# Reordering the start and the background work of a fused Fourier-mixing and MLP kernel

## The chip, the cores and the metric

The kernel runs on one core of a Trainium2 chip. The metric is device time in microseconds (us), of which less is better. Before the change it took 1956.89 us, the median of three runs (1955.35 to 1957.33). Every run of this case was in the fast state, so none had to be put aside. Profiled spans are about 1.8 us shorter than the times of the same executions (1954.8 against 1956.62 before, 1950.6 against 1952.35 after). I compare times with times and spans with spans.

Engine names in the profile: PE is TensorE, PEld is TensorE's weight load (it overlaps PE: before, they were busy for 1719.2 and 1935.8 us of a span of 1954.8), DVE is VectorE, ACT is ScalarE, POOL is GpSimd, SP is SyncE, which issues most transfers (939 of the 944 in the trace of before). A q behind a name is that engine's sequencer.

## The reference

```python
def reference(x, w_in, w_out):        # x [8, 3008, 256], w_in [256, 2048], w_out [2048, 256]
    X = np.fft.fft(np.fft.fft(x, axis=1), axis=2).real   # mixing over sequence and features
    h = X.reshape(8 * 3008, 256) @ w_in
    return np.maximum(h, 0) ** 2 @ w_out                 # out [24064, 256]
```

## The kernel before

The kernel takes the eight sequences one after the other and calls each a block of work. For each it **folds** x on VectorE (sums and differences of mirrored rows and columns), so that the Fourier transform over the sequence becomes a few smaller products with cosine and sine tables; these give Pt, Qt and Et. P's folding uses sums (`f_s`), Q's uses differences (`f_d`). The transform over the features is multiplied into w_in beforehand (G1, G2, and a column gE). Then come 48 **steps** per sequence, 384 in all: each multiplies a slice of P and Q with G (`front`), squares the positive part (`combine`) and multiplies with w_out two steps later (`back`). A regular step has 11 products, each shown as two records of TensorE, and takes 4.67 us.

```python
def fold(b, t):                      # row tile t of sequence b; returns pieces (cost, function)
    def f_s(): ...                   # VectorE: fs = x[0::2] + x[1::2]
    def f_d(): ...                   # VectorE: fd = x[0::3] - x[1:3]; asks for a later x tile
    def f_sc(): ...                  # VectorE: half of fs     (P)
    def f_dc(): ...                  # VectorE: half of fd     (Q)
    def f_w(part): ...               # VectorE: sum and difference into w
    if b == 0:
        return [f_s, f_d, f_sc, f_dc, lambda: f_w(PART[0]), lambda: f_w(PART[1])]
    ops = [(0.9, f_s), (0.9, f_d), (0.7, f_sc), (0.6, f_dc), (1.1, f_w)]
    if not odd or t == ODD0:
        return ops
    ...
    def f_sine(): ...                # ScalarE: four scalings into f1, f2
    def f_odd():                     # VectorE: w = w * turn + f1 / f2, twice
        for nm, u in (("f1", "v"), ("f2", "w")):
            nc.vector.scalar_tensor_tensor(out=st[u][rows, 1], ..., in1=st[nm][rows], ...)
    return ops + [(0.8, f_turn), (1.3, f_even), (0.2, f_sine), (1.4, f_odd)]

def fold_columns():                  # only once, in the first sequence: the middle column of all others
    nc.scalar.mul(xe, xe, 2.0)
    ...                              # VectorE: es = xe + xe, we = es +- es

def front(b, k0, n, j, between):     # two halves h; each: two products, three evictions, then side work
    for h in range(2):
        nc.tensor.matmul(hP, G1[:, fs], pt[:, ks], ...)
        nc.tensor.matmul(hQ, G2[0:P - 1, fs], qt[:, ks], ...)
        nc.vector.scalar_tensor_tensor(out=t, in0=et[:, ks], scalar=gE[:, fc:fc + 1], in1=hP, ...)
        tt(out=g[:, h, 0], in0=t, in1=hQ, op=ALU.add)
        tt(out=g[:, h, 1][:, ::-1], in0=t, in1=hQ, op=ALU.subtract)
        between()

def between():                       # a gap: emit side work for the next sequence, by listed costs
    if i < 2 * NJ or i % NJ == LAG - 1:          # NJ = 8, LAG = 2
        return
    spent -= pace                                # pace = sum of the listed costs / number of gaps
    while side and spent <= 0:
        t, f = side.pop(0)
        f()
        spent += t

# the first phase, in the order in which it is emitted
awake(44)                            # unused products, meant to keep TensorE's clock up
for_p(0); for_q(0); for_p(1)         # for_p(t): f_s, f_sc, f_w ; for_q(t): f_d, f_dc, f_w
win = [load_win(0)]                  # w_in arrives in 64 bits; VectorE and ScalarE convert it (raw)
...                                  # loads of x tiles and tables
for_p(2); rounded(0); win[0][1](); awake(2); for_p(3); groups_at(0, 5)
awake(8); for_p(4); for_p(5); for_p(6)
groups_at(3, 8, 1, 2); for_q(4); ...             # groups_at: products of P, E, Q and their joins
groups_at(9, 13, 18, 11, 12, 16, 17); for_q(1); awake(8); groups_at(14, 23)
win.append(load_win(1)); groups_at(19, 28)
copy_e = win[0][2]()                 # small product pe on TensorE
for_q(2); for_q(3); groups_at(20, 25); awake(10)
copy_e()                             # VectorE: gE = pe * 0.5
...
```

The order of the Python calls is the order of the instructions on each engine: in `e8_pe_early` below, where VectorE's copy of pe is called ahead of a weight conversion, it runs at 37.11 us and the conversion at 37.80; in the kernel after it is called behind it and runs at 41.73, the conversion at 37.46. The listed costs only spread the side work over the gaps; they time nothing.

## Time and profile before

| stage of the span | us | what bounds it |
|---|---|---|
| first phase | 0 to 66 | x landing, then VectorE and TensorE (busy 23.70 and 23.76 us of the 25 from 25 to 50) |
| first steps, with w_in and w_out converted | 66 to 115 | TensorE full, VectorE close behind |
| steps with side work for the second sequence | 147 to 227 | TensorE, with losses |
| the other sequences | 252 to 1950 | TensorE full |

The prediction below shows the lines for most of this. Two views that it leaves out turned out to matter. The first is the page's list of the costliest groups (columns: line, engine, operation, output and inputs, count, then busy us and mean ns of one, then idle us just before them and what ended most of it):

```profile
L563 PE MATMUL ph<-Pt,G 128*128 128x251 f32 (+1 forms) x1536 | 453.2, 376 | 2.3 <-DVE g L569 1.6
...
L563 PEld LDWEIGHTS ph<-Pt,G 128*128 128x128 f32 x1536 | 287.4, 189 | 41.1 <-DVE g L569 5.4
```

The second is the view of waits between 147 and 232 us (total us, times, longest):

```profile
PEld ph L563 <- DVE g L569: 4.8, 8, 1.5
...
PE ph L563 <- DVE g L569: 1.6, 3, 1.1
...
DVE w L440 <- ACT f L426: 1.4, 1, 1.4
```

Both say that the weight load of a step's first product lost more to VectorE's eviction than the product itself: 5.4 against 1.6 us over the span, and eight waits against three in this stretch. Which row shows the loss more fully is the point on which the prediction's sum for this stretch went wrong.

### The profile page before, as it was taken

How to read it: one execution, taken by the hardware profiler on the slowest of the kernel's cores; microseconds unless marked ns; L12 is line 12 of the kernel's file. 1: busy time of each engine (PE TensorE's matmuls, PEld its weight loads, DVE VectorE, ACT ScalarE, POOL GpSimd, SP SyncE). 2: the span in 40 equal slices, each digit the busy share in tenths (PEclk: the TensorE clock that was granted, in tenths of full speed). 3: DMA queues.
4: the chain of work that ended last, by engine and by line, in shares of the span. 5: the costliest groups of instructions: out<-in, count | busy, mean ns of one | idle time of the engine just before them, and what ended most of it. 6: DMA issues, size and time to landing. Idle time of an engine off the chain costs nothing.

```text
span 1954.8 us, 27739 instructions
## 1 busy us (share of the span) xinstructions
PE 1935.8 (99%) x9272; PEld 1719.2 (88%) x9272; DVE 1405.2 (72%) x3442; ACT 925.3 (47%) x1068; POOL 1168.7 (60%) x1705
## 2 busy tenths in 40 slices
PE   8999999999999999999999999999999999999998
PEld 7888888888988899888988889888898888988887
DVE  8989967777677766777667776677767777655554
ACT  1754544455444444444444454444534454444443
POOL 0046645766567665666566665666756676566664
PEclk9999999999999999999999999999999999999999
DMA  7332102111111101111011100121001101100101
GB/s 198 108 37 57 35 11 54 33 27 28 23 37 41 37 13 27 41 39 29 11 35 38 44 19 11 40 49 27 20 16 51 33 12 22 27 11 12 22 11 22
DMA packets 145341, 68.90 MB, mean 35 GB/s; under 512 B 129003, under 2 KB 136110, under 8 KB 145197
## 3 DMA queue, kind: packets, MB, share of 16 engines
q1 hardware_dynamic: 144121, 66.60, 15.1%
q8 instruction: 73, 1.20, 0.3%
q10 hardware_dynamic: 1076, 0.52, 0.1%
q14 instruction: 71, 0.58, 0.1%
HBM read 42.39 MB, written 24.68 MB: 34 GB/s over the span
## 4 chain that ended last, share of the span: by engine, by line
PE 95%; DVE 3%; DMA 1%; ACT 1%; issue 0%; POOL 0%; SPq 0%; DVEq 0%; ACTq 0%
PE ph L563 16%; PE ph L564 16%; PE mC L616 16%; PE mA L616 16%; PE mB L616 16%; PE mD L616 8%; PE pd L465 3%; PE pd L512 2%; DMA xt<-in_x_dram 1%; PE mB L603 1%; PE mA L603 1%; PE pg L269 0%; DVE w L396 0%; DVE he L566 0%; DVE g L568 0%; DVE g L569 0%
## 5 line engine op out<-in xcount | busy, mean ns | idle before, releaser
L578 ACT ACTIVATE g<-g 128x1004 f32<-128x1004 f32 (+1 forms) x384 | 399.3, 1040 | 795.5 <-DVE g L569 393.8
L586 POOL TENSOR_TENSOR s<-g 128x251 f32<-128x251 f32 (+1 forms) x376 | 245.8, 654 | 711.3 <-ACT g L579 657.1
L566 DVE SCALAR_TENSOR_TENSOR he<-Et,gE,ph 128x251 f32<-128x251 f32 (+1 forms) x768 | 362.0, 471 | 415.3 <-PE ph L564 413.3
L563 PE MATMUL ph<-Pt,G 128*128 128x251 f32 (+1 forms) x1536 | 453.2, 376 | 2.3 <-DVE g L569 1.6
L564 PE MATMUL ph<-Qt,G 127*128 127x251 f32 (+1 forms) x1536 | 452.2, 375 | 0.9 <-DVE Qt L478 0.9
L579 ACT ACTIVATE g<-g 128x1004 f32<-128x1004 f32 (+1 forms) x384 | 399.3, 1040 | 12.1
L616 PE MATMUL mC<-s,wsum 128*128 128x251 f32 (+1 forms) x1504 | 381.4, 374 | 0.0
L616 PE MATMUL mA<-g,wout 128*128 128x251 f32 (+1 forms) x1504 | 379.9, 374 | 0.0
L568 DVE TENSOR_TENSOR g<-he,ph 128x251 f32<-128x251 f32 (+1 forms) x768 | 320.5, 417 | 55.1 <-POOL s L586 1.0
L564 PEld LDWEIGHTS ph<-Qt,G 127*128 127x128 f32 x1536 | 291.8, 190 | 37.2 <-DVE Qt L478 1.3
L563 PEld LDWEIGHTS ph<-Pt,G 128*128 128x128 f32 x1536 | 287.4, 189 | 41.1 <-DVE g L569 5.4
L616 PEld LDWEIGHTS mC<-s,wsum 128*128 128x128 f32 x1504 | 285.5, 190 | 34.6
L569 DVE TENSOR_TENSOR g<-he,ph 128x251 f32<-128x251 f32 (+1 forms) x768 | 314.4, 409 | 0.0
L616 PEld LDWEIGHTS mA<-g,wout 128*128 128x128 f32 x1504 | 282.7, 189 | 35.2 <-issue 1.3
L587 POOL TENSOR_TENSOR s<-s,g 128x251 f32<-128x251 f32 (+1 forms) x376 | 281.2, 748 | 29.5
L588 POOL TENSOR_TENSOR s<-g 128x251 f32<-128x251 f32 (+1 forms) x376 | 296.0, 787 | 0.0
L589 POOL TENSOR_TENSOR s<-g,s 128x251 f32<-128x251 f32 (+1 forms) x376 | 254.7, 677 | 0.0
L616 PE MATMUL mB<-g,wsum 128*128 128x251 f32 (+1 forms) x752 | 220.5, 374 | 0.0
L616 PE MATMUL mD<-s,wout 128*128 128x251 f32 (+1 forms) x752 | 220.3, 374 | 0.0
L616 PE MATMUL mB<-s,wout 128*128 128x251 f32 (+1 forms) x752 | 219.9, 374 | 0.0
L616 PEld LDWEIGHTS mB<-g,wsum 128*128 128x128 f32 x752 | 142.6, 190 | 17.4
L616 PEld LDWEIGHTS mD<-s,wout 128*128 128x128 f32 x752 | 141.9, 189 | 17.7
(120 smaller groups left out, 1314.0 us busy)
## 6 DMA issues: line engine op xcount, KB each, us to landing
out_dram<-os SPq DMA_DIRECT2D x376, 56.0 KB
xt<-in_x_dram SPq DMA_DIRECT2D x32, 384.0 KB
xt<-in_x_dram SPq DMA_DIRECT2D x42, 128.0 KB
Et<-e_dram SPq DMA_DIRECT2D x7, 752.5 KB
xt<-in_x_dram SPq DMA_DIRECT2D x9, 512.0 KB
out_dram<-os SPq DMA_DIRECT2D x288, 6.8 KB
raw<-in_moe_w_in_dram SPq DMA_DIRECT2D x16, 256.0 KB
raw<-in_moe_w_out_dram SPq DMA_DIRECT2D x16, 256.0 KB
```

Of the source, the lines that this page charges most:

```text
L563: nc.tensor.matmul(hP, G1[:, fs], pt[:, ks], start=True, stop=True)
L564: nc.tensor.matmul(hQ, G2[0:P - 1, fs], qt[:, ks], start=True, stop=True)
L566: nc.vector.scalar_tensor_tensor(out=t, in0=et[:, ks], scalar=gE[:, fc:fc + 1], in1=hP, op0=ALU.mult, op1=ALU.add)
L568: tt(out=g[:, h, 0, 0:n], in0=t, in1=hQ, op=ALU.add)
L569: tt(out=g[:, h, 1, 0:n][:, ::-1], in0=t, in1=hQ, op=ALU.subtract)
L578: act(v, v, AF.Relu)
L579: act(v, v, AF.Square)
L586: gt(out=s1, in0=g21, in1=g22, op=ALU.add)
L587: gt(out=s2, in0=s1, in1=g11, op=ALU.subtract)
L588: gt(out=s3, in0=g11, in1=g21, op=ALU.subtract)
L589: gt(out=s4, in0=g12, in1=s2, op=ALU.subtract)
L616: nc.tensor.matmul(acc[nm][:, i, 0:n], w, v[:, 0:n], start=j == 0 and i == 0, stop=j == NJ - 1, skip_group_check=True)
```

## The change

Its intent: VectorE should fold Q's tiles 1 and 2 in the time in which it waits for x; unused products should keep TensorE's clock up there; and in the side work of all later sequences the last turn piece (`f_odd`) is held back behind three pieces of the next list, with lower listed costs for the joins. For the second sequence, four pieces are also emitted earlier, from step 10 on.

```diff
--- before.py
+++ after.py
@@ -399,7 +399,7 @@
             return [f_s, f_d, f_sc, f_dc, lambda: f_w(PART[0]), lambda: f_w(PART[1])]
         ops = [(0.9, f_s), (0.9, f_d), (0.7, f_sc), (0.6, f_dc), (1.1, f_w)]
         if not odd or t == ODD0:
-            return ops
+            return ops, None
 
 
         i = t - ODD0 - 1
@@ -440,7 +440,7 @@
                 nc.vector.scalar_tensor_tensor(out=u, in0=u, scalar=turn[rows, 0, i:i + 1], in1=st[nm][rows],
                                                op0=ALU.mult, op1=ALU.add)
 
-        return ops + [(0.8, f_turn), (1.3, f_even), (0.2, f_sine), (1.4, f_odd)]
+        return ops + [(0.8, f_turn), (1.3, f_even), (0.2, f_sine)], (1.4, f_odd)
 
     def dft_ops(b):
 
@@ -533,9 +533,9 @@
                 both(dst[:, kp:kp + 2 * n0 - 1:2], dst[:, M - kp - 2 * (nh - 1):M - kp + 1:2], st["c"],
                      st["odd"])
 
-            ops = [(0.1, even_n), (0.5, join_4), (0.7, join_2), (0.1, odd_n), (1.0, join_1)]
+            ops = [(0.1, even_n), (0.4, join_4), (0.5, join_2), (0.1, odd_n), (0.8, join_1)]
             if b and kp:
-                ops.insert(4, (0.7, join_odd))
+                ops.insert(4, (0.5, join_odd))
             return ops
 
         ops = [] if b is None else [(0.0, start)]
@@ -683,14 +683,23 @@
             nc.sync.dma_start(out=rows[full * R:], in_=part[R - rest:, full])
 
     def ahead(b):
-        folds = [piece for t in range(NT) for piece in fold(b, t)]
-        if b > 1:
-            return folds + dft_ops(b) + [(0.0, lambda: load_e(b))]
-
-        start, *groups = dft_ops(1)
-        tables = [(0.3, lambda tab=tab, i=i: part_table(tab, i)) for i in range(2) for tab in (cosT, sinT)]
-        return (folds + [start] + [(1.5, fold_columns)] + dft_ops(None) + tables
-                + groups + [(0.0, lambda: load_e(1))])
+        start, *groups = dft_ops(b)
+        if b == 1:
+
+            tables = [(0.3, lambda tab=tab, i=i: part_table(tab, i)) for i in range(2) for tab in (cosT, sinT)]
+            groups = [(1.5, fold_columns)] + dft_ops(None) + tables + groups
+        groups.insert(0, start)
+
+        pieces = []
+        for ops, last in [fold(b, t) for t in range(NT)] + [(groups + [(0.0, lambda: load_e(b))], None)]:
+            if held:
+                ops.insert(3, held.pop())
+            if last:
+                held.append(last)
+            pieces += ops
+        return pieces
+
+    held = []
 
 
     pieces = [fold(0, t) for t in range(NT)]
@@ -733,9 +742,11 @@
     awake(2)
     for_p(3)
     groups_at(0, 5)
-    awake(8)
+    awake(22)
+    for_q(1)
     for_p(4)
     for_p(5)
+    for_q(2)
     for_p(6)
     groups_at(3, 8, 1, 2)
     for_q(4)
@@ -743,14 +754,12 @@
     for_q(5)
     groups_at(10, 15, 4)
     for_q(6)
-    groups_at(9, 13, 18, 11, 12, 16, 17)
-    for_q(1)
-    awake(8)
-    groups_at(14, 23)
+    groups_at(9, 13, 18, 11, 12, 16, 17, 14)
+    awake(4)
+    groups_at(23)
     win.append(load_win(1))
     groups_at(19, 28)
     copy_e = win[0][2]()
-    for_q(2)
     for_q(3)
     groups_at(20, 25)
     awake(10)
@@ -768,9 +777,9 @@
 
 
         nonlocal spent
-        if i < 2 * NJ or i % NJ == LAG - 1:
+        if i < NJ + LAG or i % NJ == LAG - 1:
             return
-        spent -= pace
+        spent -= pace / 4 if i < 2 * NJ else pace
         while side and spent <= 0:
             t, f = side.pop(0)
             f()
@@ -811,7 +820,7 @@
             if i % per == 0:
                 assert not side
                 side = ahead(b + 1) if b + 1 < B else []
-                calls = 2 * (NJ - 1) * (len(BLOCKS) - (0 if i else 2)) - 6
+                calls = 2 * (NJ - 1) * (len(BLOCKS) - (0 if i else 2)) - 6 + (0 if i else (NJ - LAG) // 2)
                 spent, pace = 0.0, sum(t for t, _ in side) / calls
             g = front(b, k0, n, j, between)
             if i < NJ:
```

> **What bounds the kernel now.** I read the page's busy shares first, then the chain of work that ended last, then TensorE's timeline for every place where it waits, then the other engines there. The page says that one engine carries nearly the whole span:
>
> ```profile
> PE 1935.8 (99%) x9272; PEld 1719.2 (88%) x9272; DVE 1405.2 (72%) x3442; ACT 925.3 (47%) x1068; POOL 1168.7 (60%) x1705
> ...
> PE 95%; DVE 3%; DMA 1%; ACT 1%; issue 0%; POOL 0%; SPq 0%; DVEq 0%; ACTq 0%
> ```
>
> The first line is busy time by engine, the last the chain by engine. The change removes no useful matmul, so it can only win what lies between 1935.8 and the 1954.8 us of the span, plus whatever TensorE does at a lower clock. Cutting the span into stages shows where that is (columns: length, then busy us and count for TensorE, weight loads, VectorE, ScalarE, GpSimd; then TensorE's clock):
>
> ```profile
> 0.00:25.00 25.00, 20.04 (x134) 19.14 (x134) 16.20 (x45) 4.52 (x8) 0.98 (x9) 0.99 0.88 223
> 25.00:50.00 25.00, 23.76 (x117) 17.32 (x116) 23.70 (x67) 4.89 (x10) 0.00 (x0) 0.94 0.56 165
> 50.00:66.00 16.00, 13.37 (x50) 10.88 (x49) 15.47 (x38) 11.42 (x18) 0.00 (x0) 0.79 0.30 98
> 66.00:115.00 49.00, 49.00 (x241) 43.66 (x241) 46.19 (x106) 38.24 (x62) 2.73 (x4) 1.00 0.34 100
> ...
> 147.00:227.00 80.00, 78.12 (x361) 67.17 (x360) 72.50 (x161) 37.97 (x43) 52.85 (x73) 1.00 0.21 53
> ...
> 346.00:580.00 234.00, 234.00 (x1123) 209.33 (x1122) 168.81 (x414) 110.89 (x125) 150.81 (x217) 1.00 0.14 31
> ```
>
> Before 66 us TensorE waits, and from 25 us VectorE is 95% busy or more: it is the bound there. From 66 us TensorE is full; its only other losses are 1.88 us between 147 and 227 us, and half a microsecond in the tail. So two places count: the first phase, and one stretch in which the first block's steps carry the folding for the second.
>
> In the first phase VectorE itself waits for x while work that is ready stands behind in its queue (TensorE's, then VectorE's timeline; the bracket is the idle time before and its releaser):
>
> ```profile
> 18.73 1.95 PE L197 MATMUL filled<-ident 128*128 128x128 f32 x16
> 24.26 11.86 PE L465 MATMUL pd<-cosT,w 128*128 128x377 f32 x40 [3.58 <-DVE w L396]
> ...
> 16.93 0.69 DVE L366 TENSOR_TENSOR fs<-xt 128x512 f32<-128x512 f32 x1 [1.12 <-DMA xt<-in_x_dram]
> ...
> 19.09 0.69 DVE L366 TENSOR_TENSOR fs<-xt 128x512 f32<-128x512 f32 x1 [0.47 <-DMA xt<-in_x_dram]
> ...
> 22.46 0.69 DVE L366 TENSOR_TENSOR fs<-xt 120x512 f32<-120x512 f32 x1 [1.67 <-DMA xt<-in_x_dram]
> ...
> 42.09 0.16 DVE L280 TENSOR_SCALAR gE<-pe 128x2 f32<-128x2 f32 x1 [0.25 <-PE pe L278]
> ```
>
> VectorE loses 1.12 + 0.47 + 1.67 = 3.26 us; then, from 24 to 58 us, it waits only 0.25 + 0.33 us. In the later stretch this is the largest wait:
>
> ```profile
> 213.79 1.44 DVE L440 SCALAR_TENSOR_TENSOR w<-w,turn,f 128x256 f32<-128x256 f32 x2 [1.40 <-ACT f L426]
> ...
> 216.44 0.69 PE L563 MATMUL ph<-Pt,G 128*128 128x251 f32 x2 [1.08 <-DVE g L569]
> ```
>
> [...] after an idle stretch from 20.7 us the clock reads 0.67, 0.50, 0.50 and 0.62 in the four microseconds from 24, so half speed lasts some 3.4 us; after the wait before 58.6 us it reads 0.50 until 65, some 6.8 us. [...] That is the 1.40 us above: the later evictions, though ready, stood behind the odd half of the turn. [...] The pair that writes w takes 0.41 us for 127 columns in the first phase, where GpSimd is idle; in the later stretch the pair of 256 columns takes 1.50 to 1.68 us beside GpSimd, not the 0.8 that doubling would give. So side work there is dear, and where it stands matters.
>
> **The change, part by part.**
>
> *Q's folding moved.* One piece is a difference, a half and two sums: 38.61 to 40.19 us for row tile 2, 1.58 us. Tile 1's now stands after P's fourth piece, which ends at 15.73 us: 15.73 + 1.58 = 17.31, 0.38 past the arrival of the next x at 16.93. P's fifth piece (1.66 us from its start) then ends at 18.97, still before the next x at 19.09. P's sixth ends at 20.75; tile 2's piece fills 20.75 to 22.33, and x lands at 22.46. So nothing behind is delayed, and 2 x 1.58 = 3.16 us leave the VectorE-bound stretch.
>
> Not all of it arrives. I follow both queues. VectorE ends Q's last piece at 41.76 - 3.16 = 38.60. It then needs the small product pe from TensorE, which has its own row of waits: E's second odd product needs a buffer that VectorE frees at 32.59 (a time that the change does not touch), so TensorE runs 32.59 to 34.5, four unused products 0.86 to 35.4, Q's two odd products 1.9 each to about 39.3, pe 0.37 to 39.65. VectorE's gE can start at 39.85 where it started at 42.09. Gain 2.24 us; some 0.9 us is given to TensorE. One transfer is close: the first converted weight piece would be wanted at 35.4, and its bytes go through the queues until about 35.1 to 35.5. A delay up to 0.4 us there would cost about that.
>
> *More unused products.* 22 in place of 8 are 22 x 0.214 = 4.7 us, 18.73 to 23.45, with TensorE's next useful product at 24.26: they delay nothing and leave 0.8 us idle[...]. Half speed for 3.4 us cost 1.7 us of TensorE's time; but by the row above TensorE would then wait for the buffer at 32.59, so this has no gain of its own: it makes the 2.24 possible. The cut from 8 to 4 later takes 0.86 us from the row, already counted.
>
> From 42 to 58.6 us everything hangs on VectorE and ScalarE and moves by 2.24. The wait before 58.6 stays[...]. If it falls as before, the gain stays 2.24. If not, TensorE wins up to 3.4 us there but runs into VectorE: the sixth step's output weights were ready at 99.96 and used at 100.47, and VectorE's only wait for TensorE in between was 0.57, so the most is 2.24 + 0.51 + 0.57 = 3.3. I take 2.6.
>
> *The pacing.* The last turn piece of a tile now goes after three pieces of the next, so that ScalarE's four scalings (1.2 us) are done. This removes the 1.08 us wait[...]. The other two waits between 147 and 227 us (0.30 and 0.26 us[...]) came where a half and its sums stood close together: 2.4 us of side work between two evictions. The load per gap falls: with the new estimates the second block's pieces sum to 51.9 by my addition of the listed costs (55.3 before), over 53 calls (50): 0.98 for 1.11, a tenth lighter. Four pieces move earlier, into steps 10 to 15, where VectorE was busy 27.8 of 32 us and has room. But some gaps still hold 2.2 us. Of 2.1 us lost I expect 1.6 back.
>
> *Later blocks.* TensorE had no wait there: 234.00 of 234.00. Nothing to win.
>
> Sum: 2.6 + 1.6 = 4.2 us, 0.2%.
>
> **Rivals.** First, the clock falls at another place in the first phase: [...]. For it: the three times of before spread by 2 us. It moves the result by at most the 1.1 us between 2.24 and 3.3, or costs about as much if it is worse than before. Second, TensorE or the weight transfer takes the place of VectorE in the first phase, and the pulled-forward folding ends in longer waits at gE: for it, the close landing at 35 us; against it, gE would wait for TensorE until 39.85 anyway, which hides a short wait before. This would leave 1.2 us of the first part, 1954.1 in all. Third, the new pacing makes new waits: a late piece of one tile meets the pieces of the next, in a stretch where VectorE is 91% busy[...]. This would eat the 1.6 us: 1954.3. Fourth, the filling pushes back the real products if x lands earlier than in the traced run: it would have to land 0.8 us earlier, and VectorE would have to be ready for it; little speaks for that.
>
> **Range and chances.** 1956.9 - 4.2 = 1952.7. Each part may be worth 1 to 1.5 us more or less, and medians of three runs move by about 1 us: 1950.7 to 1955.2. Two per cent would be 39 us; all that TensorE loses in the whole span is under 20, so neither side is likely.
>
> **What would show it.** The changed profile should show: VectorE's waits for x under 0.6 us together; clock 1.00 from 21 to 30 us; gE near 39.9 with about 1 us of idle time before it; full TensorE from near 63 us; between 147 and 227 us under 0.8 us of TensorE waits, and none of 1 us after the turn; no waits in later blocks. The prediction is wrong if x lands later because of other traffic, if the weight conversion waits over 1 us for its bytes, if half clock lasts longer than before, or if steps 10 to 16 acquire waits from the early pieces.

## The result

| | median of six runs | range |
|---|---|---|
| before | 1956.78 us | 1955.35 to 1958.39 |
| after | 1952.14 us | 1950.96 to 1952.35 |

The ratio is 0.9975, with a 95% interval from 0.9962 to 0.9988. Ratios here are the mean time of one kernel's fast runs over the mean of the other's of the same rounds, so they are not quite the ratio of the medians. The change wins about 4.6 us. It was predicted to win 4.2 us, to 1952.7. All verdicts at 2% are "same", for this run and for every experiment; the question is only where a fifth of a per cent lies.

The page after, busy shares and chain of work by engine:

```profile
PE 1932.9 (99%) x9292; PEld 1718.5 (88%) x9292; DVE 1398.1 (72%) x3442; ACT 924.7 (47%) x1068; POOL 1172.3 (60%) x1705
...
PE 95%; DVE 3%; DMA 1%; SPq 0%; issue 0%; ACT 0%; DVEq 0%
...
L563 PE MATMUL ph<-Pt,G 128*128 128x251 f32 (+1 forms) x1536 | 451.8, 375 | 0.4 <-DVE Qt L480 0.4
...
L563 PEld LDWEIGHTS ph<-Pt,G 128*128 128x128 f32 x1536 | 287.7, 189 | 35.8 <-DVE Qt L480 0.7
```

TensorE still carries the span. The weight loads of the step's first product lost 5.3 us of idle time (41.1 to 35.8), and the wait for VectorE's eviction (5.4 us before) is no longer the releaser listed there. By stage (columns as in the prediction: length, then busy us and count of PE, PEld, DVE, ACT, POOL; then TensorE's clock, the transfers' share and GB/s):

```profile
0.00:25.00 25.00, 21.51 (x162) 20.78 (x162) 17.90 (x48) 4.52 (x8) 0.99 (x9) 1.00 0.87 220
25.00:50.00 25.00, 22.60 (x110) 16.10 (x110) 22.27 (x65) 4.89 (x10) 0.00 (x0) 1.00 0.59 168
50.00:66.00 16.00, 13.37 (x58) 11.01 (x56) 15.47 (x37) 12.78 (x21) 0.00 (x0) 0.89 0.31 98
66.00:115.00 49.00, 48.20 (x234) 42.04 (x233) 46.14 (x106) 36.96 (x60) 2.74 (x4) 1.00 0.36 100
...
147.00:227.00 80.00, 80.00 (x378) 70.96 (x377) 70.13 (x161) 41.27 (x47) 56.10 (x78) 1.00 0.20 48
...
346.00:580.00 234.00, 234.00 (x1123) 209.38 (x1122) 168.46 (x412) 110.81 (x125) 151.18 (x217) 1.00 0.14 31
```

Three things are to be seen. The clock is 1.00 up to 50 us; before it was at half from 24.3 to 27.8. From 66 to 115 us TensorE is no longer full (48.20 of 49.00). And 147 to 227 us now holds 378 products where it held 361: 17 more in the same 80 us. A regular step is 22 records in 4.67 us, 0.212 us each, so 17 are some 3.6 us (roughly, since products of the transform are of other lengths). TensorE's busy time rose only by 1.88 us there, but the weight loads' by 3.79 (67.17 to 70.96).

To measure the distance exactly I use one fixed mark per step, the start of the last product of `back` (mD<-s,wout), in both traces:

| mark | before | after | after minus before |
|---|---|---|---|
| step 8 (end of the first phase's effect) | 118.35 | 117.97 | -0.38 |
| step 16 (side work begins in earnest) | 155.87 | 155.39 | -0.48 |
| step 31 | 229.65 | 225.66 | -3.99 |
| step 43 | 302.08 | 298.22 | -3.86 |
| step 150 | 820.95 | 817.09 | -3.86 |
| step 250 | 1307.57 | 1303.32 | -4.25 |
| step 383 (the last) | 1943.70 | 1939.44 | -4.26 |

So in these two traces 3.5 us come from steps 16 to 31, 0.4 us from the later sequences, and only 0.4 us from the first phase, where 2.6 us had been expected. The later stretch first, in the view of waits from 147 to 227 us:

```profile
PEld ph L563 <- DVE g L569: 0.3, 1, 0.3
```

Eight waits have become one, and VectorE's wait for ScalarE's scalings (1.40 us before) is gone: its odd half of the turn runs without a wait.

```profile
216.97 0.87 DVE L440 SCALAR_TENSOR_TENSOR w<-w,turn,f 128x256 f32<-128x256 f32 x2
```

Now the first phase. This is VectorE's timeline after (start, length, engine, line, operation, count, idle time before it and its releaser):

```profile
5.48 0.69 DVE L366 TENSOR_TENSOR fs<-xt 95x512 f32<-95x512 f32 x1 [4.43 <-DMA xt<-in_x_dram]
...
20.45 0.69 DVE L366 TENSOR_TENSOR fs<-xt 128x512 f32<-128x512 f32 x1 [0.63 <-DMA xt<-in_x_dram]
...
23.64 0.68 DVE L366 TENSOR_TENSOR fs<-xt 120x512 f32<-120x512 f32 x1
...
37.46 0.43 DVE L241 TENSOR_SCALAR fd<-raw 128x512 uint32<-128x512 uint32 x1 [0.76 <-DMA raw<-in_moe_w_in_dram]
...
41.73 0.16 DVE L280 TENSOR_SCALAR gE<-pe 128x2 f32<-128x2 f32 x1 [1.02 <-PE pe L278]
...
48.86 0.48 DVE L566 SCALAR_TENSOR_TENSOR he<-Et,gE,ph 128x251 f32<-128x251 f32 x1 [0.33 <-PE ph L564]
```

In this execution the first x tile was folded at 5.48 us, against 4.77 in the trace of before, and the last one at 23.64 against 22.46: everything starts 0.7 to 1.2 us later. The 3.26 us of waits for x fell to 0.63. But two waits stand further down: 0.76 us for the raw bytes of the next weight piece and 1.02 us for the small product pe. So gE came at 41.73 (42.09 before) and the first eviction of step 0 at 48.86 (49.23 before): 0.37 us won. The chain of work between 24 and 50 us names what took VectorE's place:

```profile
30.84 6.53 DMA raw<-in_moe_w_in_dram
...
39.19 2.16 PE pd L465 x6
41.35 0.35 PE pe L278 x4
```

The transfer of the raw weights, then E's last joins, Q's odd product and pe lead to gE. In the repetition of after (below) the chain is another one: a piece of a cosine table lands at 26.79 us, and TensorE's own products fill the time from there to gE.

### The profile page after: what moved, and what is told of

Same layout as the page of the kernel before. It is cut to its first block, busy times and chain, and to the rows that moved or that the text cites. A ratio compares the mean times of both kernels' runs of the same rounds, so it can differ in the third digit from the quotient of the medians.

```text
span 1950.6 us, 27781 instructions
## 1 busy us (share of the span) xinstructions
PE 1932.9 (99%) x9292; PEld 1718.5 (88%) x9292; DVE 1398.1 (72%) x3442; ACT 924.7 (47%) x1068; POOL 1172.3 (60%) x1705
## 3 DMA queue, kind: packets, MB, share of 16 engines
q1 hardware_dynamic: 144121, 66.60, 15.2%
## 4 chain that ended last, share of the span: by engine, by line
PE 95%; DVE 3%; DMA 1%; SPq 0%; issue 0%; ACT 0%; DVEq 0%
PE ph L564 16%; PE mC L616 16%; PE ph L563 16%; PE mA L616 16%; PE mB L616 16%; PE mD L616 8%; PE pd L465 2%; PE pd L512 2%; DMA cosT<-in_cos_s_dram 0%; DVE m L253 0%; DVE fd L251 0%; DMA xt<-in_x_dram 0%; DMA raw<-in_moe_w_in_dram 0%; DVE he L566 0%; SPq L182 0%
## 5 line engine op out<-in xcount | busy, mean ns | idle before, releaser
L586 POOL TENSOR_TENSOR s<-g 128x251 f32<-128x251 f32 (+1 forms) x376 | 247.0, 657 | 707.5 <-ACT g L579 653.2
L563 PEld LDWEIGHTS ph<-Pt,G 128*128 128x128 f32 x1536 | 287.7, 189 | 35.8 <-DVE Qt L480 0.7
L616 PEld LDWEIGHTS mA<-g,wout 128*128 128x128 f32 x1504 | 282.9, 189 | 35.8 <-issue 1.3
L588 POOL TENSOR_TENSOR s<-g 128x251 f32<-128x251 f32 (+1 forms) x376 | 307.1, 817 | 0.0
L587 POOL TENSOR_TENSOR s<-s,g 128x251 f32<-128x251 f32 (+1 forms) x376 | 275.0, 731 | 29.5
```

Of the source, the lines that this page charges most:

```text
L563: nc.tensor.matmul(hP, G1[:, fs], pt[:, ks], start=True, stop=True)
L586: gt(out=s1, in0=g21, in1=g22, op=ALU.add)
L587: gt(out=s2, in0=s1, in1=g11, op=ALU.subtract)
L588: gt(out=s3, in0=g11, in1=g21, op=ALU.subtract)
L616: nc.tensor.matmul(acc[nm][:, i, 0:n], w, v[:, 0:n], start=j == 0 and i == 0, stop=j == NJ - 1, skip_group_check=True)
```

## The experiments

All kernels below gave correct results. Ratios are to the kernel before on the same chip: medians 1957.86 (first four kernels), 1958.0 (next four) and 1957.84 us (last four). The last eight ran on one chip, in two calls, and nine of the ten runs of before that the last four are compared with are those of the call before. Times are medians of five runs, of four for one kernel as noted. The intervals are about 0.13% wide on either side, some 2.5 us, so a single ratio tells 4 us from nothing but hardly 2 us. For smaller things I use the marks in the traces.

### The two parts apart

**First phase only** (`e1_first_only`): after, with everything outside the first phase put back.

```diff
-         if i < NJ + LAG or i % NJ == LAG - 1:
+         if i < 2 * NJ or i % NJ == LAG - 1:
-         spent -= pace / 4 if i < 2 * NJ else pace
+         spent -= pace
...                                # fold, the listed costs, ahead and the number of gaps as before, too
```

> Only the first phase of the change: Q's two pieces moved, 22 and 4 unused products; the pacing of before. Theory A (from the two traces, whose steps are 0.38 us apart at step 8 and 3.9 us apart after step 40): the first phase gives little, 0.4 to 1.6 us, and the pacing gives the rest; this kernel is 0.4 to 1.6 us faster than before, and its trace still loses about 3.6 us in steps 16 to 31. Theory B (the prediction on record): 2.6 us faster, and 2 us lost in those steps.

1956.05 us (1955.56 to 1956.69), ratio 0.9989 [0.9977, 1.0002]: 1.8 us faster by the medians, 2.2 us by the ratio. The interval holds 1, but all five runs lie below all nine of before in this call. In its trace (VectorE's timeline) the two new waits are there again, the first of them larger:

```profile
38.18 0.43 DVE L241 TENSOR_SCALAR fd<-raw 128x512 uint32<-128x512 uint32 x1 [2.16 <-DMA raw<-in_moe_w_in_dram]
...
42.45 0.16 DVE L280 TENSOR_SCALAR gE<-pe 128x2 f32<-128x2 f32 x1 [1.02 <-PE pe L278]
```

Step 8's mark is at 118.61, and from step 8 to step 43 it takes as long as before (183.72 against 183.73 us), with the eight waits of 4.8 us all present. So the first part of the change leaves steps 8 to 43 as they were.

**Pacing only** (`e2_pace_only`): after, with the first phase put back.

```diff
-    awake(22)
-    for_q(1)
+    awake(8)
...
-    for_q(2)
...
-    groups_at(9, 13, 18, 11, 12, 16, 17, 14)
-    awake(4)
-    groups_at(23)
+    groups_at(9, 13, 18, 11, 12, 16, 17)
+    for_q(1)
+    awake(8)
+    groups_at(14, 23)
...
+    for_q(2)
```

> Only the pacing: last turn piece held back, new estimates, early pieces; the first phase of before. Theory A: 3.3 to 4.0 us faster than before, no weight-load wait for VectorE in steps 16 to 31, and step 8 where it is before. Theory B: 1.6 us faster.

1954.31 us (1952.79 to 1955.92), ratio 0.9979 [0.9967, 0.9992]: 3.6 us faster by the medians, 4.1 by the ratio. From step 8 (119.86) to step 43 (300.66) it takes 180.80 us where before takes 183.73: 2.9 us of it lie there in this trace. In the view of waits, 147 to 232 us:

```profile
PEld ph L563 <- DVE g L569: 0.8, 1, 0.8
```

So the pacing is the larger part, about 3.5 us, and the first phase gives about 2 by the times of this call (the traces compared below say about 1). Their sum, 5.4 by the medians, agrees within the spread with the 4.6 of the result and the 6.2 of the repetition below.

### The filling of unused products

**Q moved, without the filling** (`e3_q_no_fill`):

```diff
-    awake(22)
+    awake(8)
```

> The changed kernel with 8 unused products in place of 22 at the wait for x. If half speed there is hidden, as TensorE must wait for a buffer anyway: within 0.5 us of the changed kernel (about 4.2 to 4.8 us faster than before), though the clock shows half speed for about 3.4 us from some 24 us on. If the filling is what the move of Q lives on: 1 us or more slower than the changed kernel.

1953.68 us (1952.62 to 1954.32), ratio 0.9976 [0.9964, 0.9989]. The clock was at half from 24.4 us for 6.83 us, and TensorE's slower products made gE wait longer (VectorE's timeline):

```profile
43.04 0.16 DVE L280 TENSOR_SCALAR gE<-pe 128x2 f32<-128x2 f32 x1 [2.46 <-PE pe L278]
```

That is 2.46 us where after had 1.02, and step 8 at 119.23 where after had 117.97. This is what the prediction said of the filling: TensorE's row, and no longer VectorE, sets gE, and a slower clock makes that row longer (38 records of its products take 11.93 us from 26.04 us on, and 10.00 from 25.91 on in the repetition of after). The times agree in sign (a median gain of 4.2 us here, 4.6 and 6.2 for after), but the ratios do not separate the two kernels.

**Filling alone** (`e4_fill_only`): before, with awake(22) in place of awake(8).

```diff
-    awake(8)
+    awake(22)
```

> The kernel before with 22 unused products in place of 8, nothing else. If half speed at 24 us is hidden: within 0.4 us of before. If it is on the path: about 1.5 us faster than before, as 3.4 us at half speed cost 1.7 us of TensorE's time.

1956.8 us (1955.71 to 1958.43), ratio 0.9993 [0.998, 1.0007]: no gain that can be told from nothing. Its clock was full at 24 us, and step 8's mark stood at 118.55, where the two traces of before have 118.35 and 119.54. In its trace gE did not wait for TensorE at all (42.77 us), where the five traces with 8 unused products and Q in its old place have waits of 0.25 to 1.14 us there: with a full clock VectorE was the bound. The median is 1.06 us below before, so a gain of that size is not excluded either.

### How much two executions of one kernel differ

**After, once more** (`e10_after_again`), without any edit, and **before, once more** (`e11_before_again`), likewise without any edit.

> The changed kernel once more, on the chip of the next three, to see how much one execution differs from another. Theory A: the landing of x and of the first converted weight differs by about 1 us between executions and moves step 8 with it, while the distance from step 8 to step 43 stays as in the first trace of it (180.25 us, against 183.73 before) within 0.1 us; 4 to 5 us faster than before.

1951.83 us (1951.52 to 1953.73), ratio 0.9973 [0.996, 0.9985]. Its x landed as late as in the first trace of after (first fold at 5.48 again), gE came at 41.05 after a wait of 1.33 us for pe, there was no wait for the raw bytes, and step 8 was at 117.25. It is 6.2 us faster than before by the medians, more than the 4 to 5 expected; from step 8 to step 43 it takes 180.24 us, as expected. Timelines of TensorE and VectorE:

```profile
25.91 10.00 PE L465 MATMUL pd<-cosT,w 128*128 128x377 f32 x38 [0.55 <-DMA cosT<-in_cos_s_dram]
...
41.05 0.16 DVE L280 TENSOR_SCALAR gE<-pe 128x2 f32<-128x2 f32 x1 [1.33 <-PE pe L278]
```

From 25.91 to the end of pe TensorE has no gap that the timeline lists, so here TensorE's own row sets gE.

> The kernel before once more, with a profile, to see how far its first trace is typical: if the first x and P's sixth x land later than in that trace (4.77 and 22.46 us), step 8 is later than 118.35 us by as much, up to 1.5 us, and the distance from step 8 to step 43 is 183.7 us again.

1957.69 us (1956.58 to 1958.03), ratio 0.9999 [0.9986, 1.0013]. Its first fold began at 5.03 us, the clock was at half for 6.83 us from 23.9, gE came at 43.75, after a wait of 1.14 us for pe, and step 8 at 119.54: 1.2 us later than in the trace that the prediction was worked out from. From step 8 to step 43 it takes 183.73 us again. The first and the last x were folded only 0.26 and 0.56 us later (5.03 and 23.02), so the landing of x is not all of the 1.2; the half clock was twice as long.

So the small gain of the first phase in the two first traces was partly an accident. Between the two repetitions, step 8 differs by 119.54 - 117.25 = 2.29 us; between the first two traces by 0.38; the clock times of the first part alone said 1.8 to 2.2. One trace of such a phase is a sample. Five traces here have the first phase of before up to step 8 (before, `e11_before_again`, `e2_pace_only`, `e5_hold_only` and `e6_pace_no_hold`): step 8 at 118.12 to 119.86, mean 118.89. Three have that of after (after, `e10_after_again`, `e1_first_only`): 117.25 to 118.61, mean 117.94. By the traces the first phase thus gives about 1 us, by the times about 2, and no more can be said.

### Does the half clock near 59 us cost anything?

**Nine more unused products in step 1's gap** (`e7_fill_gap`): after, and

```diff
         if i + 1 < NJ:
+            if i == 1:
+                awake(9)
             late.append(win[i + 1][2]())
```

> The changed kernel with nine unused products in the 2.2 us in which TensorE waits for ScalarE before the third step's small product. If the half speed that follows (3.4 us at half speed in the changed kernel's trace) is on the path: the clock stays full, and 0.5 to 1.5 us faster than the changed kernel. If VectorE sets the pace there anyway (output weights of the sixth step awaited 0.59 us at 99.1 us): within 0.3 us of it, and a longer wait at that place.

1952.16 us (1951.88 to 1954.01), ratio 0.9974 [0.9962, 0.9987]: as after. The clock now stayed full from 7.2 to 1945.9 us, so the fall was gone; but TensorE reached VectorE's output weights sooner and waited for them (TensorE's timeline):

```profile
85.23 0.69 PE L603 MATMUL mA<-g,wout 128*128 128x251 f32 x2 [0.69 <-DVE wout L254]
...
98.89 0.69 PE L603 MATMUL mA<-g,wout 128*128 128x251 f32 x2 [0.57 <-DVE wout L254]
```

With two shorter ones at 69.0 and 76.9 us these waits sum to 1.80 us, and step 8 was at 117.15, where the repetition of after in the same call had 117.25. So the half clock is hidden behind VectorE, which is the bound here before 115 us even while TensorE looks busy. The trace of the next kernel agrees: it has 6.83 us of half clock from 57.5 us, and yet that kernel has the lowest median of all.

### Taking the two new waits away

**pe earlier** (`e8_pe_early`): the small product and its copy stand ahead of Q's odd product.

```diff
     awake(4)
+    copy_e = win[0][2]()
+    copy_e()
     groups_at(23)
     win.append(load_win(1))
     groups_at(19, 28)
-    copy_e = win[0][2]()
     for_q(3)
     groups_at(20, 25)
     awake(10)
-    copy_e()
```

> The changed kernel with the small product pe, and VectorE's reading of it, ahead of Q's odd products. If the wait of 1.02 us at gE is on the path: about 1 us faster than the changed kernel, gE without a wait. If the landing of the first converted weight alone sets the pace: no change, the wait moves to Q's next piece.

1950.78 us (1950.32 to 1951.64), ratio 0.9966 [0.9953, 0.9978], against 0.9973 for after in the same call. gE now waits 0.66 us and no longer stands at the end of the phase (VectorE's timeline):

```profile
37.11 0.16 DVE L280 TENSOR_SCALAR gE<-pe 128x2 f32<-128x2 f32 x1 [0.66 <-PE pe L278]
...
37.80 0.43 DVE L241 TENSOR_SCALAR fd<-raw 128x512 uint32<-128x512 uint32 x1 [0.53 <-DMA raw<-in_moe_w_in_dram]
```

Its median is 1.05 us below that of after in the same call, and four of its five runs lie below all five of after. That is the 1 us expected, though gE still waits. The intervals overlap, so I call it a tendency.

**pe earlier, the weight conversion later, and the filling of step 1** (`e9_both`):

```diff
     awake(4)
+    copy_e = win[0][2]()
+    copy_e()
     groups_at(23)
-    win.append(load_win(1))
     groups_at(19, 28)
-    copy_e = win[0][2]()
     for_q(3)
+    win.append(load_win(1))
     groups_at(20, 25)
     awake(10)
-    copy_e()
...
+            if i == 1:
+                awake(9)
```

> A version meant to beat both: pe early, the first weight's conversion after Q's last folding piece, so that its landing (37.4 us in the changed kernel's trace) is not waited for, and the nine unused products. Theory A: up to 1.5 us faster than the changed kernel in the first phase, but the sixth step's output weights may hold it at about 0.8 us; no wait for the first weight in the trace.

1951.78 us (1951.34 to 1955.03), ratio 0.9973 [0.996, 0.9987]: a miss, no better than after. gE waited 1.41 us at 37.85 and the later conversion 0.54 us for ScalarE at 42.38; step 8 was at 117.79. Up to gE this kernel is the same as `e8_pe_early`, whose wait was 0.66; in this execution the clock had been at half for 3.41 us from 15.2. I can't tell how much of the miss is that accident and how much the edit. At the last step its trace is 1.16 us behind that of `e8_pe_early`: 0.61 of it stands at step 8, and nearly all of the rest comes between the marks of steps 19 and 20, where a weight load waits 0.85 us for VectorE's eviction.

**No waits left** (`e12_no_waits`): the product is emitted before the four unused products, its copy after E's joins, the conversion after the copy.

```diff
+    copy_e = win[0][2]()
     awake(4)
     groups_at(23)
-    win.append(load_win(1))
     groups_at(19, 28)
-    copy_e = win[0][2]()
+    copy_e()
+    win.append(load_win(1))
     for_q(3)
     groups_at(20, 25)
     awake(10)
-    copy_e()
```

> A version meant to beat both: the changed kernel with pe ahead of the four unused products, VectorE's reading of it after E's last piece, and the first weight's conversion after that, so that neither pe nor the weight's landing is waited for. Theory: 0.8 to 1.8 us faster than the changed kernel, VectorE without a wait between 26 and 47 us, and 5.5 to 7 us faster than before. If the landing of the bytes is what bounds the first phase whatever the order: no faster than the changed kernel.

1951.02 us (1950.09 to 1951.52), ratio 0.9966 [0.9953, 0.9978]. VectorE has no wait from 14 us to the first eviction of step 0, the clock is never at half between 7.2 and 1942 us, and that eviction starts 2.24 us earlier than in after's trace, and 2.61 earlier than in that of before:

```profile
46.62 0.48 DVE L566 SCALAR_TENSOR_TENSOR he<-Et,gE,ph 128x251 f32<-128x251 f32 x1 [0.32 <-PE ph L564]
```

Step 8 is at 115.69 (117.97 and 117.25 in the two traces of after, 118.35 and 119.54 in those of before). Put after E's joins, the copy finds its product done, and the conversion finds its bytes landed. By the medians this kernel and `e8_pe_early` beat both kernels of the study, by about 1 us; their intervals overlap that of after. The trace is of its fastest run (1950.09), that of `e8_pe_early` of its slowest (1951.64), so the 1.5 us between the two at step 8 say nothing of their times.

### Which half of the pacing?

**Only the last turn piece held back** (`e5_hold_only`): before, with `held` and the new `ahead`, but with the old listed costs, the old number of gaps and no early pieces.

```diff
-        return ops + [(0.8, f_turn), (1.3, f_even), (0.2, f_sine), (1.4, f_odd)]
+        return ops + [(0.8, f_turn), (1.3, f_even), (0.2, f_sine)], (1.4, f_odd)
...                                             # and ahead() with held, as in the change
```

> The kernel before with only the last turn piece held back behind three pieces of the next tile; estimates, calls and first phase of before. Theory: this removes the wait for ScalarE (1.4 us on VectorE) and with it the largest loss, 1.3 to 1.6 us of the 3.5; the weight loads' other waits for VectorE in steps 16 to 31 stay, about 2 us. If the spread of pieces matters more than their order: under 1 us.

1961.12 us (1959.14 to 1962.33), ratio 1.0017 [1.0004, 1.0031]: slower, by 3.3 us, which neither theory said. From step 16 to step 31 its trace takes 72.74 us where before takes 73.78: the wait for ScalarE is gone, and with it the 1.3 us that step 28 lost, as the first theory said, but step 30 loses 0.3 us more. By step 33 it is 6.08 us behind (245.08 against 239.00). Timelines of VectorE and TensorE in between:

```profile
236.99 0.53 DVE L344 TENSOR_TENSOR es<-xe 128x98 f32<-128x98 f32 x1 [0.67 <-ACT xe L342]
237.56 1.38 DVE L346 TENSOR_TENSOR we<-es 128x49 f32<-128x49 f32 x2
...
238.32 2.06 PE L465 MATMUL pd<-cosT,we 95*7 95x95 f32 x8 [2.51 <-DVE we L346]
```

With the turn's last piece moved, the fold of the columns comes one gap earlier, and so do the products that read it (the third line). By the order in which the kernel emits its pieces they now stand in the two gaps of one step, with only the two `front` products of one half between them; in before and in after the seven `back` products of a step stand between them as well. TensorE reaches them at 235.81, before VectorE has begun. It waits 2.51 us, and the clock falls to half from 237.8 us for 6.83 us: the mean clock from 232 to 246 us is 0.76, where before and after have 1.00. In before TensorE came to these products at 240.36, when VectorE had written what they read, and it did not wait for it.

**Everything of the pacing except the holding** (`e6_pace_no_hold`): `e2_pace_only`, but each tile keeps its last piece.

```diff
-        return ops + [(0.8, f_turn), (1.3, f_even), (0.2, f_sine)], (1.4, f_odd)
+        return ops + [(0.8, f_turn), (1.3, f_even), (0.2, f_sine), (1.4, f_odd)]
...
-         for ops, last in [fold(b, t) for t in range(NT)] + [...]:
+         for ops, last in [(fold(b, t), None) for t in range(NT)] + [...]:
```

> The kernel before with the new estimates and the earlier, lighter pace, but the last turn piece where it was. Theory: about 2 us faster than before, the five or more smaller waits gone, the wait of 1.4 us for ScalarE and about 1.3 us of loss behind it still there.

1959.94 us, median of four runs (1958.07 to 1960.31), ratio 1.001 [0.9996, 1.0024]: no gain, where about 2 us were expected. The wait of 1.4 us for ScalarE was expected to stay; it is gone, without the holding. In the first sequence its trace wins all of the pacing's 3.5 us (step 43 at 298.36, 3.72 us ahead of before). Then it loses about 0.9 us in each further sequence: 2.78 us ahead at step 100, 1.86 at 150, 1.16 at 200, 0.39 at 250, and 1.46 us behind at 340. The view of waits, 252 to 1930 us, of this kernel:

```profile
DVE w L440 <- ACT f L426: 8.5, 12, 1.3
PEld ph L563 <- DVE g L569: 6.6, 8, 1.1
PE ph L563 <- DVE g L569: 3.9, 6, 0.7
```

In the same window before had 2.1 us in 6 waits of the first kind, 0.7 us in 2 of the second and none of the third. After has neither of the first two. So VectorE's wait for ScalarE is gone from the first sequence and longer in the later ones: up to 1.3 us, where before has at most 0.3. The long ones come once in each sequence, at the last tile's `f_odd`. Why it is longer is not shown: in before, too, by the listed costs, `f_sine` and `f_odd` stand in one gap in the later sequences, so they have not come closer together.

So the two halves need each other. The lighter gaps win the first sequence, and they cost the later ones unless the last piece is held; the holding, with the old gaps, brings the columns' fold and its products too close together. Within the lighter gaps, the lower costs and the early pieces were not tested apart.

## Why the prediction was right

The time, 1952.14 against 1952.7, and the range were right. The split was not: the prediction had 2.6 us from the first phase and 1.6 from the pacing. The runs give 1 to 2 and about 3.5. The sum came out because one term was too small and the other too large, so that it agrees this well is luck, and the total alone proves little.

**The pacing: mechanism right in the main, size wrong, 3.65 us lost and not 2.1.** The step that failed is the one that took "the other two waits between 147 and 227 us" and the wait of 1.08 as the whole loss. I counted the three waits in which TensorE's matmul row is idle (1.08, 0.30 and 0.26 us, 1.64 in all) and put them at 2.1: 1.24 for the first, as the products around it start 1.67 us apart in the trace (214.77 and 216.44) where 0.43 is usual, and about 0.45 for each of the others (0.89 and 0.85 us apart). The weight-load row showed eight, of 4.8 us. The term that was mis-sized is that of the other waits, 0.9 us by my count; the wait of 1.08, put at 1.24, was nearly right. The marks show it: a regular step takes 4.67 us from mark to mark, and before took longer in seven of them.

| from step | to step | excess over 4.67 us |
|---|---|---|
| 16 | 17 | 0.56 |
| 18 | 19 | 0.35 |
| 20 | 21 | 0.52 |
| 25 | 26 | 0.34 |
| 27 | 28 | 0.19 |
| 28 | 29 | 1.34 |
| 30 | 31 | 0.35 |

The sum is 3.65 us: 1.34 with the wait for ScalarE (from step 28) and 2.31 without it. The weight loads' row moved more than the matmuls': from 147 to 227 us the matmuls' busy time rose by 1.88 us, the weight loads' by 3.79, while steps 16 to 31 became 3.5 us shorter. After takes (225.66 - 155.39) / 15 = 4.68 us per step there, and the 4.8 us of waits shrank to 0.3. "I expect 1.6 back" of 2.1 was also too careful: nearly all of it came back. What removed which part differs from what I wrote. The holding alone does remove the wait for ScalarE (`e5_hold_only`), but so do the lighter gaps alone (`e6_pace_no_hold`, 70.26 us from step 16 to step 31, as after). The holding is needed in the later sequences, where I had expected nothing. The rival that a late piece of one tile meets the pieces of the next did not occur in after; 80.00 of 80.00 us are busy. The one wait of a weight load that is left, between the marks of steps 19 and 20, is 0.3 us there but 0.8 to 0.9 in `e2_pace_only`, `e7_fill_gap` and `e9_both`, which take 70.8 us for these steps.

**Q's folding moved: mechanism right, gain too large, and with a large spread.** The waits for x fell from 3.26 to 0.63 us, nearly as expected ("under 0.6 us together"). gE then waited 1.02 us for TensorE (predicted: about 1). What failed is the next step, TensorE's row of products before gE: the prediction let E's second odd product start at 32.59 us, when VectorE frees its buffer, "a time that the change does not touch". It started at 33.90 and 33.75 in the two traces of after. In the first, VectorE freed the buffer that late (x had landed 1.2 us later). In the repetition TensorE had no gap from 25.91 us on, and the chain goes back along its products to a piece of a cosine table that landed at 26.79: its own row was the bound, and the prediction left the table's landing out. Already in before TensorE had no gap from 24.26 us to gE, and gE waited for it in all five traces with that first phase, so "from 25 us VectorE is 95% busy or more: it is the bound there" was only half of it. "A delay up to 0.4 us there would cost about that" measured 0.76 in after, 2.16 in the first part alone and nothing in the repetition, so the second rival, that TensorE or the weight transfer takes VectorE's place, occurred. The prediction put gE at 39.85, 2.24 earlier than before; the two traces have 41.73 and 41.05, which is 0.36 earlier between the first traces, 2.70 between the repetitions, and 1.26 between the means of the five and the three traces above. I took one trace of before for a property of the kernel. The times give 1.8 to 2.2 us for the part, the marks at step 8 about 1, where I had 2.24 without the clock and took 2.6.

**The unused products: right.** The clock stayed full from 21 to 50 us, and without them gE waited 2.46 us in place of 1.02. Alone they gave nothing that shows (0.9993). How much they are worth in time beside the moved folding stays open: the trace says 1.3 us at step 8 (119.23 against 117.97), and the ratios 0.9976 and 0.9973 to 0.9975 do not separate.

**The wait before 58.6 us: right in its outcome.** The clock (the "it" of the prediction's "If it falls as before") fell to half in after too, for 3.41 us and not 6.83. I had given this up to 1.1 us. The run that filled it shows that it is worth nothing: VectorE's output weights are the next bound. The trace of after has that wait as well, 0.59 us at 99.71 (TensorE's timeline), the sixth step's output weights that the prediction had named as the limit:

```profile
99.71 0.69 PE L603 MATMUL mA<-g,wout 128*128 128x251 f32 x2 [0.59 <-DVE wout L254]
```

So full TensorE "from near 63 us", which the prediction asked for, did not hold: 48.20 of 49.00 from 66 us.

**Later blocks: nearly right.** "Nothing to win" held for the busy share, 234.00 of 234.00; the marks gain 0.39 us between steps 150 and 250. Before had 0.7 us of weight-load waits there and after none, again in the row that I had not read. What the prediction did not see at all is that half of the pacing, by itself, would lose 5.2 us there (from 3.72 ahead to 1.46 behind).

The rival of the filling pushing back real products did not occur: TensorE's unused products ended at 24.6 us, the first real one followed at once, and the next waited 0.35 us for a table to land, so nothing was lost by it.

Three readings in the prediction need a correction or a number. The wait before 58.6 us, after which the clock fell, is 2.17 us in its own trace (TensorE's timeline of before), while the idle stretch from 20.7 us is 3.58; more on this in the last section. An unused product takes 0.223 us from start to start in the traces of before and after, not 0.214, so 22 of them took 4.91 us (19.57 to 24.48 in after). And the pairs that write w in the later stretch take 1.07 to 1.74 us over all seven of them, not 1.50 to 1.68; the 0.41 of the first phase is from the pair's start to the next instruction's, and 0.49 to its own end. That GpSimd makes them slow is not shown: no run took GpSimd's work away.

## What to carry to other kernels

When a matmul row is nearly full, read its weight-load row too, and measure a step's length between fixed marks: here the matmul row showed only about half of the loss (1.88 us in that row, 3.65 by the marks). Before a gain of 2 us is worked out from transfers that land in one trace, ask how much that stage moves between executions of the same code; here step 8 moved by up to 1.7 us, as much as the stage's gain. And when side work is spread by listed costs, a change of one cost moves every later piece: test the parts apart, in all stages, since half of a good change can be a loss by itself.

## What else the traces showed

- How long the clock stays at half: 3.41 us (from 24.3 us in before, from 59.2 in after) or 6.83 us (from 58.5 in before, from 237.8 in `e5_hold_only`), apart from the fall in the last steps. The length of a wait did not by itself tell whether the clock falls. Falls came with an idle stretch of TensorE of 3.58 us (before, 20.68 to 24.26), of 2.51 us (`e5_hold_only`, 2.0 us after it began, 235.81 to 237.8) and of 2.17 us (before and after, at the wait before the third step's small product). None came with 2.12 us in after (12.99 to 15.11), nor in `e3_q_no_fill` with 2.16 us at that same wait (57.35 to 59.51; its clock is 1.00 from 50 to 66 us). What decides between them is not shown.
- In which of TensorE's two rows single losses are to be read: here the matmul row listed 3 waits of 1.6 us and the weight-load row 8 of 4.8 us, the truth by the marks being 3.65 us, so neither row's waits are the loss.
- How much a load's landing differs at the start between executions of one program: the first x tile was folded at 4.77 and 5.03 us in two traces of the same kernel, and the last at 22.46 and 23.02.
